# Attention scores from stacked high and low keys over 128 rows, in a decay-attention and two-layer expert kernel

## The chip, the cores and the metric

The kernel runs on one core of one Trainium2 chip. The metric is the device time of one execution in microseconds (us), as the median of several runs. A core has TensorE (PE in the profile, with PEld for its weight loads), VectorE (DVE), ScalarE (ACT), GpSimd (POOL) and SyncE (SP, which issues the DMAs here). All times below come from the runs and from one profiled execution of the kernel before.

## The reference

Decay attention over 4 batches, 8 heads, 576 positions and head size 64; then two expert layers over 2304 tokens (4 x 576), width 512, inner width 2048. Cut to what matters:

```python
def _attn_ref(q, k, v, f):
    scores = (1 / sqrt(64)) * q @ k.T
    cum = np.cumsum(np.log(np.clip(f, 1e-4, 1.0)), axis=-1)
    decay = cum[:, :, :, None] - cum[:, :, None, :]
    scores = np.where(causal, -1e9, scores + decay)
    attn = exp(scores - max(scores)); attn /= sum(attn) + 1e-9
    return attn @ v

def _moe_ref(x, w_in, w_out, alpha):
    h = x @ w_in
    return (np.maximum(h, 0) + alpha * np.minimum(h, 0)) @ w_out

def _moe2_ref(x, w_in, w_out):          # beta = 1
    h = x @ w_in
    return np.where(h >= 1, h, np.where(h <= -1, 0, (h + 1) ** 2 / 4)) @ w_out
```

The expert weights arrive as 64-bit floats and are turned into 32-bit values on the chip.

## The kernel before

**Precision.** PE takes two kinds of 32-bit operands here. Plain F32 products appear in the trace as two products and loads per call; F32R ("fp32r") appear as one. Where F32R is used, each operand is split into a high part (a cast on ACT) and a low part (the difference, on DVE), and three products are summed: high x high, high x low, low x high.

**Attention.** Scores are computed transposed: keys on the 128 output partitions, queries along the columns. Each batch has two units of queries: 0 to 255 ("even") and 256 to 575 ("odd", 320 queries); there are 8 units and each runs over 4 pairs of heads. A pair loads K, Q and V of two heads side by side (2 x 64 = 128 columns), transposes K and Q on PE (L469), copies them out of PSUM on ACT (L476) and, from batch 1 on, makes low parts on DVE (L479). So the two heads of a pair lie on partitions 0 to 63 and 64 to 127, and a score product of one head uses 64 rows only. An even unit has key blocks of 256 and 128 query columns per head, an odd one of 320, 320, 320, 192 and 64. Batch 0 ("plain") uses F32 for everything; in later batches the last block of a head is F32 (L616) and the others are three F32R products (L619). The last key block of an odd unit has 64 keys only.

Per block: score products into one of 2 PSUM buffers, eviction to S on ACT (L633), causal mask on POOL (L420) if it touches the diagonal. Per head: the first block plus its decay bias gives Mx on ACT (L653); each further block is added its bias and maximised into Mx on DVE (L662); POOL reduces Mx over partitions (L669); DVE subtracts bias and maximum from each block (L685); ACT takes the exponential (L690). From batch 1 on, P is split (PH on ACT L700, PL on DVE L704, one buffer each) and multiplied with V (L730 to L732); small blocks and batch 0 use F32 (L724). A column of ones in V gives the sums. Per pair: the results leave PSUM (L766, L767), the sums go through two DMA trips for the reciprocals, DVE multiplies (L795), and ACT and DVE write the high and low parts of the expert input x (L804, L807).

**Expert layers.** Tokens go in 9 chunks of 256, each in 16 slices of the inner width: ps_h (L930, 12 products), the activation on DVE and ACT, ps_y (L988, 12 products); layer 2 is L1077 and L1120. x has a ring of three chunks: x of chunk c can be written only after the ps_h of chunk c-3. Weights are loaded as 64-bit words and converted by ACT and DVE (L849 to L886), 32 pieces a layer; the last 8 pieces of layer 1 go through a ring of 2 staging buffers, and layer 2 opens its buffers when attention has ended. A second memory pool ("phase 2", with split P and V and the split K and Q) opens when layer 1 is converted and batch 0's PV is done.

**Order.** Nothing is ordered by hand. A planner (Order.emit) takes tasks with an engine, an estimated duration, a position, dependencies and buffer rings, and emits each engine's instructions in the order of its own model of time: among the tasks that are ready on an engine, the one with the lowest position. Attention lies ahead of the expert slices by position, so PE takes expert slices when no attention task is ready. Engines then run their queues in that order.

## Time and profile before

| | us |
|---|---|
| median of 3 runs | 1183.98 |
| lowest, highest | 1183.69, 1185.22 |
| the profiled execution | 1185.71 |
| its span, first to last instruction | 1183.9 |

The profile comes from one execution. Busy shares say how long an engine had an instruction in work; the chain of waits follows what ended last back in time; the timeline shows single instructions; a table by stage gives busy times for chosen stretches. Matmul ends are modelled in the profile, so differences between starts, as the chain shows them, are a better measure of a product than its own duration. In the shape of a product, 64\*128 means 64 rows of the array.

### The profile page before, as it was taken

The numbers are of one execution on the slowest core, as the hardware profiler recorded it, in microseconds if no ns is written. First come the engines' busy times: TensorE is split into PE (matmuls) and PEld (weight loads), VectorE is DVE, ScalarE is ACT, GpSimd is POOL, SyncE is SP. The second block draws the span as 40 slices with busy tenths as digits, with TensorE's granted clock in tenths as the row PEclk, the third lists the DMA queues.
The fourth block names the chain that finished last, engine by engine and source line by source line (L and its number), as shares of the span: only waits on it lengthen the run. The fifth ranks groups of instructions, "written<-read, shape, count | busy, mean of one in ns | idle before, by whom it ended". The sixth has DMA issues, their size and how long they took to land.

```text
span 1183.9 us, 20711 instructions
## 1 busy us (share of the span) xinstructions
PE 1126.8 (95%) x7357; PEld 984.6 (83%) x7357; DVE 792.6 (67%) x1892; ACT 615.3 (52%) x1622; POOL 216.9 (18%) x328
## 2 busy tenths in 40 slices
PE   4869988999999999999999998889999999999998
PEld 2436788888888888988889998778999999999997
DVE  4887877677776777657765869997544544444443
ACT  5766754666666657656554435554333333333332
POOL 2512301322332232312210006331000000000000
PEclk9999998999999999999999999999999999999999
DMA  7661122222112122121100623351000010000000
GB/s 198 183 218 36 36 78 78 51 52 55 37 43 74 36 46 49 39 64 42 36 25 8 199 90 120 120 156 38 28 27 19 18 37 19 19 19 1 19 19 18
DMA packets 125656, 72.37 MB, mean 61 GB/s; under 512 B 89424, under 2 KB 119120, under 8 KB 125552
## 3 DMA queue, kind: packets, MB, share of 16 engines
q1 hardware_dynamic: 125552, 71.04, 21.8%
q8 instruction: 58, 0.95, 0.3%
q14 instruction: 46, 0.38, 0.1%
HBM read 61.42 MB, written 9.51 MB: 60 GB/s over the span
## 4 chain that ended last, share of the span: by engine, by line
PE 84%; DVE 8%; DMA 3%; issue 2%; ACT 2%; SPq 1%; POOL 1%; DVEq 0%; ACTq 0%; POOLq 0%
PE ps_h L930 17%; PE ps_y L988 16%; PE ps_z L1120 16%; PE ps_h L1077 15%; PE ps_s L619 6%; PE ps_o L724 5%; PE ps_s L616 4%; PE pst L469 2%; DVE val L867 2%; PE ps_o L730 1%; DVE val L872 1%; DMA raw<-in_moe_w_in_dram 1%; PE ps_o L732 1%; PE ps_o L731 1%; DVE val L852 1%
## 5 line engine op out<-in xcount | busy, mean ns | idle before, releaser
L930 PE MATMUL ps_h<-x,w 128*128 128x256 f32 x1728 | 241.6, 290 | 6.8 <-ACT w L880 4.2
L988 PE MATMUL ps_y<-gH,w 128*128 128x256 f32 x1152 | 240.6, 292 | 3.1 <-ACT gH L948 3.1
L1077 PEld LDWEIGHTS ps_h<-x,w 128*128 128x128 f32 x1728 | 225.5, 191 | 19.2 <-DVE g L1088 8.2
L1077 PE MATMUL ps_h<-x,w 128*128 128x256 f32 x1728 | 230.6, 283 | 4.5 <-DVE g L1088 4.4
L930 PEld LDWEIGHTS ps_h<-x,w 128*128 128x128 f32 x1728 | 219.3, 193 | 16.9 <-ACT w L880 4.4
L988 PEld LDWEIGHTS ps_y<-gH,w 128*128 128x128 f32 x1152 | 189.3, 191 | 12.9 <-issue 4.4
L1120 PE MATMUL ps_z<-w,gH 128*128 128x512 f32 x576 | 180.8, 395 | 0.8 <-ACT gH L1093 0.8
L988 PE MATMUL ps_y<-gL,w 128*128 128x256 f32 x576 | 164.2, 285 | 4.4 <-DVE gL L951 4.3
L1085 ACT ACTIVATE g<-g,half 128x256 f32<-128x256 f32 x144 | 73.3, 509 | 130.7 <-DVE g L1082 130.3
L1096 DVE TENSOR_TENSOR gL<-g,gH 128x256 fp32r<-128x256 f32 x144 | 61.8, 429 | 94.7 <-ACT gH L1093 94.7
L633 ACT COPY S<-ps_s 128x320 f32<-128x320 f32 (+3 forms) x224 | 77.3, 348 | 83.0 <-PE ps_s L619 47.6
L1093 ACT CAST gH<-g 128x256 fp32r<-128x256 f32 x144 | 58.3, 405 | 112.8 <-PE ps_z L1120 104.5
L420 POOL TENSOR_SCALAR_AFFINE_SELECT S<-S 128x128 f32<-128x128 f32 (+1 forms) x160 | 59.1, 375 | 309.9 <-ACT S L633 306.0
L988 PEld LDWEIGHTS ps_y<-gL,w 128*128 128x128 f32 x576 | 110.4, 192 | 6.3 <-DVE gL L951 5.8
L1088 DVE TENSOR_TENSOR g<-ps_h,g 128x256 f32<-128x256 f32 x144 | 61.0, 423 | 81.0 <-ACT g L1085 81.0
L1120 PE MATMUL ps_z<-w,gL 128*128 128x512 f32 x288 | 112.1, 389 | 0.8 <-DVE gL L1096 0.8
L1120 PEld LDWEIGHTS ps_z<-w,gH 128*128 128x128 f32 x576 | 99.0, 190 | 13.6 <-ACT gH L1093 1.0
L669 POOL PARTITION_ALL_REDUCE Mb<-Mx x64 | 85.6, 1338 | 65.5 <-DVE Mx L662 54.7
L685 DVE SCALAR_TENSOR_TENSOR S<-Mb,nb,S 128x320 f32<-128x320 f32 (+3 forms) x224 | 91.5, 457 | 6.0 <-POOL Mb L669 6.0
L724 PE MATMUL ps_o<-S,vF 64*128 64x64 f32 (+4 forms) x256 | 79.1, 401 | 16.9 <-issue 11.4
L948 ACT CAST gH<-g 128x256 fp32r<-128x256 f32 x144 | 58.5, 407 | 68.9 <-DVE g L943 58.7
L662 DVE SCALAR_TENSOR_TENSOR Mx<-S,nb,Mx 128x320 f32<-128x320 f32 (+3 forms) x160 | 69.6, 435 | 33.8 <-POOL S L420 15.2
(96 smaller groups left out, 1679.7 us busy)
## 6 DMA issues: line engine op xcount, KB each, us to landing
raw<-in_moe_w_in_dram SPq DMA_DIRECT2D x32, 512.0 KB
raw<-in_moe_w_out_dram SPq DMA_DIRECT2D x32, 512.0 KB
x<-ysb SPq DMA_DIRECT2D x36, 128.0 KB
x<-x SPq DMA_DIRECT2D x9, 512.0 KB
out_dram<-osb SPq DMA_DIRECT2D x18, 256.0 KB
qr<-in_q_dram SPq DMA_DIRECT2D x64, 64.0 KB
kr<-in_k_dram SPq DMA_DIRECT2D x32, 128.0 KB
vr<-in_v_dram SPq DMA_DIRECT2D x24, 128.0 KB
```

The lines of the kernel that those rows point to most:

```text
L619: nc.tensor.matmul(out=o, lhsT=aa[rows, ks], rhs=qs_.t[cc][rows, qo:qo + m], start=(t == 0), stop=(t == 2))
L633: nc.scalar.copy(out=Sb.t[:, so:so + m], in_=sb.t[:, :m])
L662: nc.vector.scalar_tensor_tensor(out=mo, in0=Sb.t[:, so:so + m], scalar=bias, in1=mo, op0=ALU.add, op1=ALU.max)
L669: nc.gpsimd.partition_all_reduce(Mb.t[:, :n], Mx.t[:, :n], P, ReduceOp.max)
L685: nc.vector.scalar_tensor_tensor(out=sl, in0=Mb.t[:, qo:qo + m], scalar=nb[:, kb, hd:hd + 1], in1=sl, op0=ALU.subtract, op1=ALU.subtract)
L724: nc.tensor.matmul(out=o, lhsT=vf, rhs=Sb.t[:ks, off - g0:off - g0 + m], start=(kb == 0), stop=last)
L930: nc.tensor.matmul(out=hb.t, lhsT=a[:, sl], rhs=b, start=(cc == 0 and t == 0), stop=(cc == NCC - 1 and t == 2))
L988: nc.tensor.matmul(out=Y[c][e // 2][:, e % 2, :], lhsT=a[:, sl], rhs=b, start=(s == 0 and t == 0 and e % 2 == 0), stop=(s == NF - 1 and t ...
L1077: nc.tensor.matmul(out=hb.t, lhsT=a[:, sl], rhs=b, start=(cc == 0 and t == 0), stop=(cc == NCC - 1 and t == 2))
L1085: nc.scalar.activation(out=gb.t, in_=gb.t, func=AF.Square, scale=0.5, bias=half)
L1096: nc.vector.tensor_tensor(out=gg.t[1], in0=gb.t, in1=gg.t[0].bitcast(F32), op=ALU.subtract)
L1120: nc.tensor.matmul(out=zb[tg].t, lhsT=a[:, sl], rhs=b, start=(s == 0 and t == 0), stop=(s == NF - 1 and t == 2))
```

## The change

- K of one head is stacked over 128 partitions: its high part on the head's own 64, its low part on the other 64 (khi, klo). Q is loaded twice per head and transposed once per head, so that each head has the same Q on both halves, split in high and low (qhi, qlo). A score block is then two F32R products of 128 rows, (high and low K) x high Q and (high and low K) x low Q, for every block and every batch; the two F32 forms and the three-product form are gone.
- K buffers: a ring of two, one per head, in the first attention pool. Q: a ring of two there and a third in phase 2. S: six buffers there and a seventh in phase 2, instead of eight.
- The decay bias is added in the eviction (ACT, Identity with a bias per partition). Mx starts as the maximum of the first two blocks on DVE (and, in even units, a copy on ACT of the columns that only the first block has); the later maxima and the subtraction take two tensors and no bias.
- The last key block is padded with zeros to 128 keys, in K, Q, and V, so its transposes and its PV product have 128 rows.
- In the conversion of layer 1, the intermediate values lie in the piece's own weight buffer.
- The planner's estimates for products and for the reduction on POOL are changed.

The diff, cut:

```diff
     def pe(n, cnt=1):
-        return cnt * (max(n, 256) / 2.4 + 3)
+        return cnt * (max(n, 240) / 2.4 + 13)
...
-        raw=2, qr=1, qp=1, q=2, k0=1, k3=1, kF=1, kE=1, S=8, M=3, r=1, PH=1, PL=1, s=2, o=2, h=2, g=4, gg=LH + 1,
-        stage=2, sums=1, rec=1, val=2, raw2=NRAW, val2=NVAL, x2r=1, z0=1, z1=1, osb=3).items()}
+        raw=2, qr=1, q=2, k=2, S=6, M=3, r=1, PH=1, PL=1, s=2, o=2, h=2, g=4, gg=LH + 1,
+        stage=2, sums=1, rec=1, raw2=NRAW, val2=NVAL, x2r=1, z0=1, z1=1, osb=3).items()}
...
+            R["q"].slots.append(None)
+            R["S"].slots.append(None)
...
         def load_q(qb_=qb_, b=b, pr=pr, q0=q0, q1=q1):
-            qb_.t = ap1.tile([P, 3, 2, D], F32, tag="qr", name="qr")
-            load_tok(qb_.t, q, b, pr, q0, q1)
+            qb_.t = QR
+            for x in range(2):
+                load_tok(qb_.t[:, :, :, x, :], q, b, pr, q0, q1)
...
+        kx = [Buf(R["k"]) for _ in range(2)]
...
+            a = last["ktr"] = add("PE", 112 * (t1 - t0) // P, ktr, p0 - 1, [T["lk"], last.get("ktr")],
+                                  new=[pb] + (kx if t0 == 0 else []), use=[kb_] + ([] if t0 == 0 else kx))
+            for j in range(2):
+                hr = slice(j * D, (j + 1) * D)
+                lr = slice(D - j * D, 2 * D - j * D)
+
+                def khi(j=j, hr=hr, pb=pb, t0=t0, t1=t1, k_of=k_of):
+                    nc.scalar.copy(out=k_of(j)[hr, t0:t1], in_=pb.t[hr, :t1 - t0])
+
+                def klo(j=j, hr=hr, lr=lr, pb=pb, t0=t0, t1=t1, k_of=k_of):
+                    nc.vector.tensor_tensor(out=k_of(j)[lr, t0:t1], in0=pb.t[hr, :t1 - t0],
+                                            in1=k_of(j)[hr, t0:t1].bitcast(F32), op=ALU.subtract)
...
-                    for t, (aa, cc) in enumerate(((kx.t[0], 0), (kx.t[0], 1), (kx.t[1], 0))):
-                        nc.tensor.matmul(out=o, lhsT=aa[rows, ks], rhs=qs_.t[cc][rows, qo:qo + m],
-                                         start=(t == 0), stop=(t == 2))
...
+                    for t in range(2):
+                        nc.tensor.matmul(out=sb.t[:, :m], lhsT=kt.t[:, kb * P:(kb + 1) * P],
+                                         rhs=qt.t[t][:, qo:qo + m], start=(t == 0), stop=(t == 1))
...
-                    nc.scalar.copy(out=Sb.t[:, so:so + m], in_=sb.t[:, :m])
+                    nc.scalar.activation(out=Sb.t[:, so:so + m], in_=sb.t[:, :m], func=AF.Identity, bias=bias)
...
+                nc.vector.tensor_tensor(out=Mx.t[:, f0:f0 + fm], in0=S0[0].t[:, S0[1] + f0:S0[1] + f0 + fm],
+                                        in1=S1[0].t[:, S1[1]:S1[1] + fm], op=ALU.max)
...
-                        nc.vector.scalar_tensor_tensor(
-                            out=sl, in0=Mb.t[:, qo:qo + m], scalar=nb[:, kb, hd:hd + 1], in1=sl,
-                            op0=ALU.subtract, op1=ALU.subtract)
+                        nc.vector.tensor_tensor(out=sl, in0=Mb.t[:, qo:qo + m], in1=sl, op=ALU.subtract)
...
-            pool = ph["stage"] if layer == 1 else P2["p"]
-            vb.t = pool.tile([P, DM], F32, tag=f"val{vb.slot}", name="val")
+            pool, tag = (wpool, f"w{i}") if layer == 1 else (P2["p"], f"val{vb.slot}")
+            vb.t = pool.tile([P, DM], F32, tag=tag, name="val")
```

## Rows read from the trace of the kernel before

**Rows 1.** The page, part 1: busy us, share of the span, instructions of each engine.
```profile
PE 1126.8 (95%) x7357; PEld 984.6 (83%) x7357; DVE 792.6 (67%) x1892; ACT 615.3 (52%) x1622; POOL 216.9 (18%) x328
```

**Rows 2.** Busy us by stage: length, engines, granted PE clock, DMA share, GB/s.
```profile
100.00:193.00 93.00, 85.97 (x521) 70.64 (x521) 73.68 (x166) 59.90 (x157) 14.17 (x24) 0.93 0.21 56
193.00:630.00 437.00, 436.36 (x3055) 382.36 (x3054) 311.31 (x823) 280.00 (x835) 121.13 (x228) 1.00 0.20 47
...
705.00:830.00 125.00, 111.64 (x795) 101.73 (x794) 116.03 (x221) 65.05 (x141) 47.74 (x32) 1.00 0.35 106
```

**Rows 3.** Chain of waits, 384 to 399 us: start us, us, engine and line.
```profile
386.82 0.63 PE ps_s L619 x3
387.45 1.62 PE ps_h L930 x12
...
390.47 0.51 PE ps_s L619 x3
...
392.61 0.36 PE ps_s L616 x2
392.97 0.48 PE pst L469 x3
393.45 1.44 PE ps_h L930 x12
...
398.28 0.15 PE ps_o L731
```

**Rows 4.** Timeline: x written (L807, L804), chunks 1 and 6 leaving PSUM (L1005).
```profile
269.11 0.49 DVE L807 TENSOR_TENSOR x<-r,x 128x192 fp32r<-128x192 f32 x2
...
279.28 0.38 ACT L1005 COPY ysb<-ps_y 128x256 f32<-128x256 f32 x1 [0.53 <-PE ps_y L988]
...
353.59 0.55 DVE L807 TENSOR_TENSOR x<-r,x 128x192 fp32r<-128x192 f32 x2
...
600.55 0.41 ACT L804 CAST x<-r 128x256 fp32r<-128x256 f32 x1 [1.24 <-PE ps_h L930]
...
657.17 0.73 DVE L807 TENSOR_TENSOR x<-r,x 128x64 fp32r<-128x64 f32 x2
...
665.33 0.37 ACT L1005 COPY ysb<-ps_y 128x256 f32<-128x256 f32 x1 [0.74 <-PE ps_y L988]
```

**Rows 5.** Chain of waits, 193 to 630 us: shares by line.
```profile
by line: PE ps_y L988 30.4%; PE ps_h L930 30.2%; PE ps_s L619 15.6%; PE ps_o L724 5.4%; PE pst L469 4.5%; PE ps_s L616 4.0%; PE ps_o L730 3.9%; PE ps_o L732 2.9%; PE ps_o L731 2.9%; issue 0.1%; ACT r L767 0.1%; ACT sums L766 0.1%; ACT S L63
```

**Rows 6.** Groups by line, whole span: busy us, mean ns | idle before, releaser.
```profile
L930 PEld LDWEIGHTS ps_h<-x,w 128*128 128x128 f32 x1728 | 219.3, 193 | 16.9 <-ACT w L880 4.4
```

**Rows 7.** Groups by line and form, DVE, 193 to 630 us.
```profile
L685 DVE SCALAR_TENSOR_TENSOR S<-Mb,nb,S 128x320 f32<-128x320 f32 x72 | 36.3, 547 | 0.0
...
L479 DVE TENSOR_TENSOR qL<-pst,qH 128x320 fp32r<-128x320 f32 x12 | 5.8, 484 | 0.3 <-ACT qF L476 0.3
...
L795 DVE TENSOR_TENSOR r<-r,sums 128x320 f32<-128x320 f32 x10 | 4.9, 490 | 6.0 <-DMA sums<-spread 5.9
```

**Rows 8.** Groups by line and form, ACT, 193 to 630 us.
```profile
L633 ACT COPY S<-ps_s 128x320 f32<-128x320 f32 x72 | 30.4, 424 | 32.3 <-PE ps_s L619 30.3 <-DVE PL L704 1.4 <-PE ps_o L724 0.3
...
L653 ACT ACTIVATE Mx<-S,nb 128x320 f32<-128x320 f32 x24 | 13.5, 561 | 0.8
...
L476 ACT CAST qH<-pst 128x320 fp32r<-128x320 f32 x12 | 5.1, 427 | 0.4
```

**Rows 9.** Chain of waits, 91 to 103 us.
```profile
96.48 1.36 PE ps_s L616 x2
...
99.71 2.86 PE ps_h L930 x12
```

**Rows 10.** The end of layer-1 conversion and batch 1's first transposes and x.
```profile
191.45 0.68 DVE L886 TENSOR_TENSOR w<-raw,w 128x512 fp32r<-128x512 f32 x1
...
192.46 0.44 PE pst L469 x4
...
224.94 0.49 DVE L807 TENSOR_TENSOR x<-r,x 128x192 fp32r<-128x192 f32 x2
```

More of the change, by code (lines that the diff above doesn't have):

```diff
@@ L328, in xt @@
         return X[c]
-    assert all(blocks_of(q0, q1)[0][-1][2] <= P for _, q0, q1 in units)
-    KC = 3 * P
+    KC = 4 * P
     V = {}
@@ L356, in open_phase @@
             nc.gpsimd.memset(tf[:, :, 1, :], 0.0 if nm == "vL" else 1.0)
+            if nm == "vF" and S % P:
+                for x in (0, 2):
+                    nc.gpsimd.memset(t[S % P:, cnt - 1, x, :], 0.0)
     open_phase(1)
+    RAW = [ap2.tile([P, NKB, 2, D], F32, name=f"raw{i}") for i in range(2)]
+    QR = ap1.tile([P, 3, 2, 2, D], F32, name="qr")
+    for t in RAW:
+        nc.gpsimd.memset(t[S % P:, NKB - 1], 0.0)
+    nc.gpsimd.memset(QR[S % P:, 2], 0.0)
     def load_tok(dst, src, b, pr, t0, t1):
@@ L454 @@
         T["lk"] = add("SP", 2.85 * nk, load_k, p0 - 3, [last.get("lv"), last.get("lk")], new=[kb_])
         last["lk"] = T["lk"]
-        T["lq"] = last["lq"] = add("SP", 2.85 * n, load_q, p0 - 3, [last.get("lq")], new=[qb_])
-        qs_ = Buf(R["qp" if plain else "q"])
-        def transposes(src, t0, t1, parts, deps, uses, new, pos):
-            m_ = t1 - t0
+        T["lq"] = last["lq"] = add("SP", 5.7 * n, load_q, p0 - 3, [last.get("lq")], new=[qb_])
+        nsplit = sum(y[2] > PVF for y in blocks)
@@ L469, in tr @@
                     nc.tensor.transpose(
-                        pb.t[:, c * P:c * P + m],
-                        src.t[:m, t0 // P + c, :, :].rearrange("p j d -> p (j d)"), ident[:m, :m])
-            a = add("PE", 112 * -(-m_ // P), tr, pos, deps + uses, new=[pb] + new, use=[src])
-            for a0, a1, dstH, dstL, to in parts:
-                def hi(a0=a0, a1=a1, dstH=dstH):
-                    nc.scalar.copy(out=dstH(), in_=pb.t[:, a0:a1])
-                def lo(a0=a0, a1=a1, dstH=dstH, dstL=dstL):
-                    nc.vector.tensor_tensor(
-                        out=dstL(), in0=pb.t[:, a0:a1], in1=dstH().bitcast(F32), op=ALU.subtract)
-                h = add("ACT", act(a1 - a0), hi, pos, [a], use=[pb] + new)
-                to.append(h)
-                if dstL is not None:
-                    to.append(add("DVE", dve(a1 - a0), lo, pos, [h], use=[pb] + new))
@@ new lines, with qtr, qhi, qlo @@
+        qx, qready = [], [[], []]
+        for j in range(2):
+            pb, qb = Buf(R["s"]), Buf(R["q"])
+            qx.append(qb)
+            np_ = -(-n // P)
+            def qtr(pb=pb, qb_=qb_, j=j, np_=np_):
+                pb.t = ps_a.tile([P, 512], F32, tag=f"s{pb.slot}", name="pst")
+                for c in range(np_):
+                    nc.tensor.transpose(
+                        pb.t[:, c * P:(c + 1) * P], qb_.t[:, c, j].rearrange("p x d -> p (x d)"), ident)
+            def qhi(pb=pb, qb=qb, n=n):
+                pool = ap1 if qb.slot < 2 else ph["p"]
+                qb.t = [pool.tile([P, NMAX], F32R, tag=f"q{x}{qb.slot}", name=f"q{x}") for x in "HL"]
+                nc.scalar.copy(out=qb.t[0][:, :n], in_=pb.t[:, :n])
+            def qlo(pb=pb, qb=qb, n=n):
+                nc.vector.tensor_tensor(out=qb.t[1][:, :n], in0=pb.t[:, :n], in1=qb.t[0][:, :n].bitcast(F32),
+                                        op=ALU.subtract)
+            a = add("PE", 112 * np_, qtr, pos_of(2 * pr + j) - 1, [T["lq"], last.get("qtr")], new=[pb], use=[qb_])
+            last["qtr"] = a
+            h = add("ACT", act(n), qhi, pos_of(2 * pr + j) - 1, [a], new=[qb], use=[pb])
+            qready[j] = [h, add("DVE", dve(n), qlo, pos_of(2 * pr + j) - 1, [h], use=[pb, qb])]
@@ L671 @@
             last["par2"] = last.get("par")
-            pa = last["par"] = add("POOL", 400 + 6.3 * n, par, pb_, [mt, last["par2"]], new=[Mb], use=[Mx])
+            pa = last["par"] = add("POOL", 1150, par, pb_, [mt, last["par2"]], new=[Mb], use=[Mx])
             ob = Buf(R["o"])
@@ L722, in pv @@
                         if plain or small:
-                            vf = V["vF"][:ks, kb - v0].rearrange("p a d -> p (a d)")[:, cs]
-                            nc.tensor.matmul(out=o, lhsT=vf, rhs=Sb.t[:ks, off - g0:off - g0 + m], start=(kb == 0), stop=last)
+                            vf = V["vF"][:, kb - v0].rearrange("p a d -> p (a d)")[:, cs]
+                            nc.tensor.matmul(out=o, lhsT=vf, rhs=Sb.t[:, off - g0:off - g0 + m], start=(kb == 0), stop=last)
                             return
@@ L890, in convert @@
         if wide:
-            a = add("ACT", act(DM), mag, pos, [a], new=[vb], use=[rb])
+            a = add("ACT", act(DM), mag, pos, [a] + (wdeps if layer == 1 else []), new=[vb], use=[rb])
             a = add("DVE", dve2(DM), clamp, pos, [a], use=[vb])
```

139 lines of the change are left out of this document (43 added, 96 removed).

## The prediction

> **What bounds the kernel now.** I read the page's busy shares first: PE 95% of the span, DVE 67%, ACT 52% [rows 1]. One mean over stages says little, so the table by stage comes next [rows 2]. From 193 to 630 us, while the attention of batches 1 to 3 is mixed with the first expert layer, PE is busy 436.4 of 437 us, DVE 311 (71%), ACT 280 (64%). From 705 to 830 it is the other way round: DVE 116 of 125 us, PE 112; there the layer-2 weights are converted. Before 193 it is mixed (100 to 193: PE 92%, DVE 79%). So an edit to scores is worth what it takes from PE between 193 and 630, if attention and DVE let the PE have it.
>
> Second, the chain of waits at one place [rows 3]. A 64-row score block (three products, 320 columns) takes 0.63 us, one of 192 columns 0.51, the two-pass-pair small block (L616) 0.36. The third product of a full-row PV triple takes 0.15. Of 0.63 only about 3 x 0.15 = 0.45 is streaming: some 0.18 is paid on entering 64-row mode. The group of 12 expert products behind a score block takes 1.62, but 1.44 behind full-row transposes: 0.18 again on leaving. Neither is a wait on another engine.
>
> Third, who is late at the chunk borders [rows 4]. The last x of unit 2, which chunk 2 needs, is written at 269.1, and chunk 1 leaves PSUM at 279.3; unit 3's last x comes at 353.6. In unit 7, x for chunk 8 is written at 600.6 only after ps_h of chunk 5 frees the ring of three (the row names PE ps_h as releaser), so there the attention waited for PE. The last x comes at 657.2, and chunk 6 leaves its PSUM at 665.3, the 2 to 3 slices by which y trails h: about as at 269. At both places the expert layer had no further chunk to go to: attention is late. PE is thus the limit in the middle, and the attention's own chain at both ends.
>
> **Scores.** Batches 1 to 3 hold 24 heads with 7 blocks each, 168 blocks: 24 of 256 columns, 72 of 320, and 24 each of 192, 128 and 64. The chain gives L619 15.6% and L616 4.0% of 437 us [rows 5], 85.7 us with the entering cost. Leaving adds at most 168 x 0.18 = 30 us, charged to expert and PV groups; I take 27, since few score blocks stand next to another 64-row piece. After the change a block is two full-row products. 320 columns: 2 x 0.146 = 0.29 us [rows 3], 72 x 0.29 = 21 us. For 256 columns and fewer I take 1.44/12 = 0.12 us a product, 96 x 0.24 = 23 us. No row shows an fp32r product of 64 or 128 columns: below, 192 columns are no dearer than that; above, four passes as in L616 would add about 0.1 us to each 128-column product, 5 us in all. I take the former, nearest in form. Sum 44 us.
>
> **Transposes.** K stays at 5 or 2 a pair (the tail padded to 128); Q is transposed per head, from two copies, 6 instead of 3 for an odd unit (320 queries) and 4 instead of 2 for an even one. That is 12 x 3 + 12 x 2 = 60 more, at 0.48/3 = 0.16 us [rows 3]: 9.5 us. So PE loses 85.7 + 27 - 44 - 9.5 = 59 us of work. Per odd pair: 6 x 0.34 + 2 x 0.27 + 2 x 0.12 + 10 x 0.18 - 0.5 = 4.1 us; an even pair keeps the rest, (59 - 49)/12 = 0.8, say 1 us.
>
> The trace puts 12 full-row products, each with its own weights, into 1.44 us, so the loads are hidden [rows 3]. The Trainium skill, "TensorE: Matmul & The Clock Gate", Part 3, What overlaps and what doesn't, says that a weight load overlaps a running product only if the row groups differ, which two full-row products never do. By that rule each of 336 products would show a load, which would eat the gain; here the trace disagrees with it, and the fourth rival prices it.
>
> **DVE.** L479 now makes the low part of K and Q once per head. At 484 ns for 320 columns, 1.5 ns a column [rows 7], an odd pair goes from 832 to 1920 columns (+1.6 us), an even one from 384 to 1024 (+1.0): 31 us in batches 1 to 3. The decay bias leaves L662 and L685, which become two-tensor operations: 547 to about 489 ns at 320 columns [rows 7], 0.058 x 288 = 17 us back. Net +14: 325 of some 390 us, 83%. In batch 0, which had no low parts, it is +18 - 6 = +12 us.
>
> **ACT.** Eviction with bias: 561 instead of 424 ns [rows 8], 168 x 0.137 = +23 us. The first maximum (L653) goes: 48 x some 0.53 = -26 (561 ns at 320 columns, less at 256); even units copy 128 columns instead, 24 x an estimated 0.25 = +6. High parts at 427/320 = 1.33 ns a column: odd 960 to 1920 columns, even 640 to 1024, 21 us. Net +24: 304 of 390 us, 78%.
>
> **SP and buffers.** Q is loaded twice, 80 issues more. From 193 to 630 the DMA share is 0.20 [rows 2], which covers them, and I cost them at nothing (without that cover a pair would wait for its Q); in the first 60 us they stand in SP's order before the v loads that PV waits for, so there they belong to the bound of the start below. S falls from 8 buffers to 6, then 7; two K buffers must both be free before the next pair's transposes, so the longer preparation (ACT +1.3, DVE +1.6 us odd; +0.5, +1.0 even) may stand between the scores of one pair and the next. Queued behind it on ACT are evictions and exponentials, on DVE the low parts of P, and PV waits for those.
>
> **Start, 0 to 193.** Scores of 320 columns take 1.36 us there and 12 expert products 2.86 [rows 9], half pace. PE saves over 20 us, but the stretch ends with the layer-1 conversion: DVE writes the last low part at 191.5, and the PE runs batch 1's transposes at 192.5, behind it [rows 10]. Conversion fills the DVE's gaps, and DVE gets 12 us more. I take 0, between 12 lost (all on the path) and 10 won (attention ends earlier and leaves DVE to conversion).
>
> **193 to 355.** Attention is late here. PE per pair: 4 x 4.1 + 4 x 1 = 20 us; all preparation in series would take back 4 x 2.9 + 4 x 1.5 = 18. So 2 to 20 us; I take 12. Also, K, Q and six S buffers no longer lie in the second pool, so batch 1's first scores need not wait for the conversion, and the 33 us from there to its first x at 224.9 [rows 10] shrink: 0 to 10, I take 6.
>
> **355 to 601.** PE is late. 6 odd and 8 even pairs: 33 us; 28 after some loss to fuller DVE and ACT queues (20 to 33).
>
> **601 to 658.** Chain-bound: 4 us (0 to 8). Afterwards, 2 chunks x 16 slices x 2 x 1.44 = 92 us of expert work and the DVE-bound conversion only shift.
>
> Sum: 0 + 18 + 28 + 4 = 50 us. The profiled execution took 1185.7 (span 1183.9 and 1.8 around it); 1135.7 against it, and as the median of the runs is 1.7 lower, **1134.0 us**.
>
> **The rivals.** (1) PE gets all of it: 59 us, with up to 10 of the start and some of the waiting in 705 to 830 hidden: about 1118. For it: PE idle is nil in 193 to 630, and the 100-to-193 stage keeps PE at 92% with DVE at 79%. Against: the late x at 269 and 657.
>
> (2) Attention's chain or DVE paces everything: only half comes, 1160. For it: DVE at 83% in the mean, and no slack at 269 and 657.
>
> (3) Slower: the longer preparation of K and Q stands in series between pairs and x comes later. Price 18 us before 355 and 3 x 2.9 = 9 us after 601, the middle's gain idle because the next chunk's x is missing: about 1210. It decides when less than 2.9 of the 4.6 us of scores saved per odd pair lies on the attention's chain. Against: score blocks stand in one queue with everything, and the next pair's transposes begin while PV still runs. S at 7 for 8 belongs here: evictions of 320 columns waited only 1.4 us in all for a freed S (releaser DVE PL) [rows 8].
>
> (4) The change doesn't do what it says: loads in the open. A load is 0.193 us long [rows 6], and 336 x 0.193 = 65 us would cancel the 59: 1185 to 1190. The 1.44 us groups speak against it.
>
> **How the numbers follow.** Forecast (1122 to 1148) 0.44, rival 1 0.22, rival 2 0.19, rival 3 0.09, rival 4 0.06. The bounds of all terms give gains of 10 to 81 us; leaving out rivals 3 and 4 and the outer ends, the range is 1106 to 1170. A change of 0.2% (2.4 us) is about what a measurement can tell from none. Faster 0.86, same 0.05, slower 0.09.
>
> **What would show it.** In the chain after: score blocks of 0.29 and 0.24 us, no 64-row form among the products, every group of 12 at 1.44 us, and PE below full in places between 193 and 355. L633 near 560 ns, L685 near 490. Attention's last x near 605 to 610 instead of 657; the end of layer-1 conversion within 12 us of 191. I am wrong if the last x moves by less than 20 us while PE shows gaps (chain-bound), if conversion ends later than 205, or if two full-row products take over 0.4 us.

## The result: slightly slower, 1192.6 us

| | before | after |
|---|---|---|
| median of the runs on the same chip, us | 1184.07 | 1192.56 |
| lowest, highest | 1183.69, 1185.22 | 1192.32, 1194.44 |
| span of the profiled execution | 1183.9 | 1190.9 |

The ratio after to before is 1.0073, 95% interval 1.0056 to 1.0091. The forecast was 1134.0, the range 1106 to 1170. Neither held it; to "slower" the text gave 0.09.

The page of the kernel after, part 1, which answers [rows 1]:

```profile
PE 1063.2 (89%) x7317; PEld 982.2 (82%) x7317; DVE 827.6 (69%) x1992; ACT 635.2 (53%) x1614; POOL 208.8 (18%) x334
```

PE lost 63.6 us of work over the whole run. The forecast had 59 for batches 1 to 3 and "over 20" for batch 0, some 80 together, so the size was too large by some 16 us. Yet the span grew by 7.0, so PE now stands idle for some 71 us more. The table by stage, after, says where (the second, third and fifth line answer [rows 2]; columns as there):

```profile
0.00:100.00 100.00, 47.74 (x161) 33.91 (x162) 75.92 (x174) 63.80 (x149) 24.01 (x45) 0.78 0.68 186
100.00:193.00 93.00, 78.57 (x533) 68.76 (x533) 85.80 (x205) 68.97 (x180) 21.92 (x30) 0.96 0.28 71
193.00:630.00 437.00, 408.15 (x3123) 394.45 (x3123) 327.38 (x882) 289.45 (x809) 113.28 (x223) 0.96 0.23 53
...
600.00:660.00 60.00, 52.02 (x408) 51.30 (x407) 40.19 (x105) 32.04 (x87) 9.97 (x17) 0.93 0.17 46
...
705.00:830.00 125.00, 104.46 (x714) 94.98 (x713) 115.99 (x206) 59.34 (x126) 46.09 (x32) 0.96 0.34 104
830.00:1191.00 361.00, 357.21 (x2261) 323.55 (x2259) 171.99 (x406) 125.24 (x281) 0.00 (x0) 1.00 0.06 20
```

From 193 to 630 PE was busy without a gap before; now it has 29 us of gaps, and in 705 to 830 it works 104.5 us instead of 111.6 while DVE is as full as it was (116.0 in both). The timeline of DVE, after, for the answer to [rows 4] and [rows 10]: the last low part of layer 1's weights (L863), and the last x of units 1, 2 (first pair), 3 and 7 (L784):

```profile
192.73 0.69 DVE L863 TENSOR_TENSOR w<-raw,w 128x512 fp32r<-128x512 f32 x1
...
196.08 0.55 DVE L784 TENSOR_TENSOR x<-r,x 128x256 fp32r<-128x256 f32 x2
...
212.48 0.49 DVE L784 TENSOR_TENSOR x<-r,x 128x192 fp32r<-128x192 f32 x2
...
354.73 0.64 DVE L784 TENSOR_TENSOR x<-r,x 128x192 fp32r<-128x192 f32 x2
...
657.20 0.73 DVE L784 TENSOR_TENSOR x<-r,x 128x64 fp32r<-128x64 f32 x2 [0.36 <-ACT x L781]
```

The last x comes at 657.20; before it came at 657.17 [rows 4]. The attention, with some 60 us less of PE work beside and in it, did not finish earlier at all, and the stretch from the last x to the end grew by 7 us, from 526.7 to 533.7 (span less the start of the last x). The chain of waits after, in one odd pair (batch 1), shows both what worked and what didn't:

```profile
305.38 0.14 PE ps_s L591 x2
305.52 1.51 PE ps_y L965 x12
...
307.47 0.44 PE pst L487 x4
...
308.51 1.49 PE ps_y L965 x12
310.00 1.44 PE ps_h L907 x12
311.44 1.44 PE ps_y L965 x12
...
313.32 0.31 PE ps_s L591 x2
...
315.90 0.29 PE ps_s L591 x2
316.19 1.44 PE ps_y L965 x12
...
318.07 0.29 PE ps_s L591 x2
```

A block of 320 columns takes 0.29 to 0.31 us, as forecast, for 0.63 [rows 3], and the group of 12 behind it 1.44 instead of 1.62. But blocks come 1.7 to 2.6 us apart, since expert groups stand between them, and from the last block of one pair (305.4) over the transposes of the next pair's K (307.5) to its first block (313.3) it is 8 us. An odd pair took 21 to 28 us here (x at 276.8, 302.3, 330.0 and 354.7 in unit 3), where the kernel before needed 19 to 23 (x at 288.4, 307.5, 330.8, 353.6). One pair is not much to go by, so take the nine borders from one odd pair of batches 1 to 3 to the next odd pair. From the start of a pair's last score product to the start of the next pair's first one, the mean is 4.3 us in the kernel before and 9.2 us in the kernel after (from the starts of PE's products in the two traces).

### The profile page after: what moved, and what is told of

The parts are those of the page before. It is cut to its first block, busy times and chain, and to the rows that moved or that the text cites. A ratio compares the mean times of both kernels' runs of the same rounds, so it can differ in the third digit from the quotient of the medians.

```text
span 1190.9 us, 20943 instructions
## 1 busy us (share of the span) xinstructions
PE 1063.2 (89%) x7317; PEld 982.2 (82%) x7317; DVE 827.6 (69%) x1992; ACT 635.2 (53%) x1614; POOL 208.8 (18%) x334
## 4 chain that ended last, share of the span: by engine, by line
PE 59%; DVE 12%; issue 11%; DMA 9%; ACT 4%; SPq 3%; POOL 2%; POOLq 0%; DVEq 0%; ACTq 0%
PE ps_z L1097 16%; PE ps_h L1054 16%; PE ps_h L907 10%; PE ps_y L965 9%; DMA sums<-spread 4%; PE ps_s L591 3%; DVE val L844 2%; DMA spread<-rec 2%; PE ps_o L701 2%; DVE val L829 1%; DMA raw<-in_moe_w_in_dram 1%; SPq L377 1%; DVE val L849 1%; POOL Mb L648 1%; PE ps_o L709 1%
## 5 line engine op out<-in xcount | busy, mean ns | idle before, releaser
L1054 PEld LDWEIGHTS ps_h<-x,w 128*128 128x128 f32 x1728 | 226.6, 192 | 20.7 <-DVE g L1065 9.6
L907 PEld LDWEIGHTS ps_h<-x,w 128*128 128x128 f32 x1728 | 226.9, 198 | 16.2 <-ACT x L781 8.1
L605 ACT ACTIVATE S<-ps_s,nb 128x320 f32<-128x320 f32 (+3 forms) x224 | 99.6, 448 | 46.5 <-PE ps_s L591 44.2
L1065 DVE TENSOR_TENSOR g<-ps_h,g 128x256 f32<-128x256 f32 x144 | 61.1, 424 | 82.5 <-ACT g L1062 82.5
L701 PE MATMUL ps_o<-S,vF 128*128 128x64 f32 (+4 forms) x256 | 72.8, 381 | 26.8 <-ACT r L744 8.2
L591 PE MATMUL ps_s<-qH,kT 128*128 128x320 f32 (+3 forms) x224 | 75.1, 335 | 22.4 <-ACT S L605 8.3
L667 ACT ACTIVATE S<-S 128x320 f32<-128x320 f32 (+1 forms) x192 | 78.1, 423 | 27.6 <-DVE S L664 25.5
L648 POOL PARTITION_ALL_REDUCE Mb<-Mx x64 | 78.2, 1222 | 76.8 <-ACT Mx L632 29.6
```

The lines of the kernel that those rows point to most:

```text
L591: nc.tensor.matmul(out=sb.t[:, :m], lhsT=kt.t[:, kb * P:(kb + 1) * P], rhs=qt.t[t][:, qo:qo + m], start=(t == 0), stop=(t == 1))
L605: nc.scalar.activation(out=Sb.t[:, so:so + m], in_=sb.t[:, :m], func=AF.Identity, bias=bias)
L648: nc.gpsimd.partition_all_reduce(Mb.t[:, :n], Mx.t[:, :n], P, ReduceOp.max)
L667: ex = add("ACT", act(gn), lambda Sb=Sb, gn=gn: nc.scalar.activation(out=Sb.t[:, :gn], in_=Sb.t[:, :gn], func=AF.Exp, scale=-SCALE), pb_, ...
L701: nc.tensor.matmul(out=o, lhsT=vf, rhs=Sb.t[:, off - g0:off - g0 + m], start=(kb == 0), stop=last)
L907: nc.tensor.matmul(out=hb.t, lhsT=a[:, sl], rhs=b, start=(cc == 0 and t == 0), stop=(cc == NCC - 1 and t == 2))
```

## The experiments

Every run of an experiment was compared with the kernel before on the same chip; times are medians, ratios are to the kernel before. The kernel after is at 1.0073. Beside the experiments the kernel before took 1185.8 to 1187.2 us, beside the kernel after 1184.1, so times from different comparisons agree to about 3 us. "The gap" below is the mean over the nine borders just described; "the rest" is the time from the last x to the end of the profiled execution.

**First theory: K's preparation stands in series.** Both K buffers come free only after a pair's last score block. Its rivals, numbered as the expectations of the runs name them and not as in the prediction: (1) seven S buffers for eight; (2) the longer eviction; (3) the second Q load; (4) the planner's estimates; (5) batch 0's preparation on DVE. Four runs.

*K transposed once for each head* (the loop over heads goes outside):

```diff
-        for t0 in range(0, nkp, KC):
+        for j in range(2):
+            for t0 in range(0, nkp, KC):
...
-            a = last["ktr"] = add("PE", 112 * (t1 - t0) // P, ktr, p0 - 1, [T["lk"], last.get("ktr")],
-                                  new=[pb] + (kx if t0 == 0 else []), use=[kb_] + ([] if t0 == 0 else kx))
+                a = last["ktr"] = add("PE", 112 * (t1 - t0) // P, ktr, kpos, [T["lk"], last.get("ktr")],
+                                      new=[pb] + ([kx[j]] if t0 == 0 else []), use=[kb_] + ([] if t0 == 0 else [kx[j]]))
```

> The changed kernel, but K is transposed once for each head, each head's K buffer being freed and refilled by itself. Theory 1 (the preparation of K stands in series between pairs, because both K buffers come free only after the pair's last score block): the next pair's first K is made while the second head's scores run, the gap of some 6.5 us between the score phases of odd pairs (323.5-331.5 scores, next K transposes at 333.5, next scores some 6 us later) shrinks to about 2; 12 odd pairs in batches 1 to 3 would give 12 x 4 = 48 us, of which the expert layer can take no more than PE's idle time from 193 to 630 (437 - 408 = 29 us) less the added transposes (12 x 5 + 12 x 2 = 84 at 0.16 us, 13 us): 1165 to 1180. Rival 1 (seven S buffers for eight) and rival 2 (bias in the eviction lengthens the score ring): the gap is not what paces, 1190 to 1200.

Measured: 1185.94, ratio 0.9991 (0.9972 to 1.001), between the bands of the two theories: some 7 us better than the kernel after, 6 short of what theory 1 wanted. The trace says more than the time. The gap is 5.0 us instead of 9.2 and the last x comes at 638.00, 19 us earlier, as theory 1 has it; but the rest takes 548 us instead of 534, so most of that gain is lost again behind the last x (the edit adds 13 us of transposes to PE).

*Three K buffers, two Q buffers from batch 1 on:*

```diff
-            R["q"].slots.append(None)
+            R["k"].slots.append(None)
```

> The changed kernel with three K buffers from batch 1 on and two Q buffers instead of three (the space allows no more). Both K buffers of a pair are then free as soon as the previous pair's first head has its scores. Theory 1: as K made by head, without its extra transposes: 1160 to 1178. Rival 1 and rival 2: no gain, 1190 to 1200, as K's buffers are not what a pair waits for.

Measured: 1172.16, ratio 0.9881 (0.9844 to 0.9918). The chain of this kernel at the same place:

```profile
306.61 0.29 PE ps_s L591 x2
...
307.23 0.29 PE ps_s L591 x2
...
309.17 0.29 PE ps_s L591 x2
309.46 0.22 PE pst L487 x2
309.68 1.42 PE ps_h L907 x12
...
314.04 0.14 PE ps_s L591 x2
...
316.41 0.24 PE ps_s L591 x2
```

The next pair's K is transposed (L487 at 309.5) while this pair's blocks still run; its first block (0.24 us, so 256 columns: the next unit's) is at 316.4, 2.4 us after the last one. Unit 3's pairs end at 275.2, 301.4, 318.8 and 338.5, so two of them take 17 to 20 us, and the last x comes at 625.55, 32 us earlier. The gap is 4.9 us.

This holds in every kernel of the study, whatever its order. The gap is 3.8 to 4.3 us in the four with the old form of K, 8.5 to 10.8 in the eleven with two buffers that come free together, and 3.6 to 5.8 in the five with a third buffer or K made by head. So two buffers make the gap, and it costs the attention time. What that is worth at the end is another matter: here 32 us at the last x became 20 us in all, since the rest grew from 534 to 545 us.

*Eight S buffers instead of seven, two Q buffers; and the kernel before with six and seven:*

```diff
-            R["q"].slots.append(None)
-            R["S"].slots.append(None)
+            R["S"].slots.append(None)
+            R["S"].slots.append(None)
```

> The changed kernel with eight S buffers from batch 1 on, as before the change, and two Q buffers instead of three. Rival 1 (a head's four S groups, with seven slots, wait for the head before; the kernel before had room for two whole heads): 1165 to 1180, last x before 640. Theory 1: 1189 to 1196, odd pairs stay at 25 us.

Measured: 1193.63, ratio 1.005 (1.003 to 1.0069), last x at 658.9.

> The kernel before with six S buffers, seven from batch 1 on, as in the changed kernel; nothing else. Rival 1: slower by 5 us or more, 1189 to 1205, odd pairs longer than the 20 to 21 us they take before. Theory 1: within 2 us of 1184.

Measured: 1179.56, ratio 0.9935 (0.9912 to 0.9959). In neither kernel did the number of S buffers cost time that could be seen; the first of the two edits also takes one Q buffer away, so only the second tests S alone. The rival has nothing that speaks for it. That the kernel before got faster by 0.65% with less space was expected by no theory, and was the first sign that another order by itself moves the time.

**The parts by themselves.** *The bias part alone, in the kernel before; and the kernel after without it:*

```diff
-                    nc.scalar.copy(out=Sb.t[:, so:so + m], in_=sb.t[:, :m])
+                    nc.scalar.activation(out=Sb.t[:, so:so + m], in_=sb.t[:, :m], func=AF.Identity, bias=bias)
...
-                        nc.vector.scalar_tensor_tensor(
-                            out=sl, in0=Mb.t[:, qo:qo + m], scalar=nb[:, kb, hd:hd + 1], in1=sl,
-                            op0=ALU.subtract, op1=ALU.subtract)
+                        nc.vector.tensor_tensor(out=sl, in0=Mb.t[:, qo:qo + m], in1=sl, op=ALU.subtract)
```

> The kernel before with one part of the change: the decay bias is added in the scores' eviction, the first maximum joins two blocks on DVE, the later maxima and the subtraction become two-tensor operations. S stays at eight, the scores stay 64-row products. If the bias part is harmless (theory 1 puts the loss on K's preparation): 1178 to 1187, L685 near 490 ns, the eviction near 560 ns. Rival 2 (the longer eviction sits in the ring of two score tiles, so every block comes later): 1189 or more, and x of units 3 and 7 later than 353.6 and 657.

Measured: 1176.93, ratio 0.9914 (0.989 to 0.9938). The subtraction at 320 columns, by line and form from 193 to 630 us, takes 494 ns instead of 547 [rows 7]:

```profile
L692 DVE TENSOR_TENSOR S<-Mb,S 128x320 f32<-128x320 f32 x72 | 32.5, 494 | 0.7 <-POOL Mb L676 0.7
```

and the table by stage of the same kernel shows the work taken off: DVE 295.8 us instead of 311.3 [rows 2], ACT 277.8 instead of 280.0.

```profile
193.00:630.00 437.00, 436.62 (x3056) 383.25 (x3056) 295.78 (x817) 277.76 (x807) 118.04 (x222) 1.00 0.19 45
```

> The changed kernel with the bias part taken back: plain eviction, the first maximum on ACT with the bias, the later maxima and the subtraction with the bias as a scalar. Keys stacked, queries held twice, S at six and seven. Theory 1: no faster than the changed kernel, 1189 to 1200 (DVE gets back 17 us of work). Rival 2: 1172 to 1185.

Measured: 1200.38, ratio 1.011 (1.0086 to 1.0134). Both directions go the same way: without the bias part the time is longer. But 8 and 10 us are no more than another order alone can move (below), so that the part helps isn't shown. Nothing shows that the longer eviction costs time, and that rival has nothing that speaks for it.

*K by head with three buffers:* the two edits above together.

> Three K buffers, two Q buffers, and K transposed once for each head, so a head's K can be made one and a half heads ahead. If K's preparation still holds up the attention with three buffers: 1155 to 1168, last x before 615. If DVE and ACT (84 and 76 of 100 us in the stages) pace it by now: 1170 to 1178, as the 84 added transposes of 0.16 us are 13 us more of PE and nothing else moves.

Measured: 1188.6, ratio 1.0016 (0.9999 to 1.0033), last x at 644.8: far from both bands. The finer division with more space is 16 us slower than three buffers alone, although nothing of what theory 1 names is missing: the gap is 5.0 us. Its 84 more transposes are 13 us of PE, and they pass through the two PSUM buffers that the scores use; which of this or the order cost it was not separated.

*Each query loaded once* (scores then hold one half of their terms). The edit also halves the planner's estimate of the load, so the order of the work changes too:

```diff
-            for x in range(2):
-                load_tok(qb_.t[:, :, :, x, :], q, b, pr, q0, q1)
+            load_tok(qb_.t[:, :, :, 0, :], q, b, pr, q0, q1)
...
-        T["lq"] = last["lq"] = add("SP", 5.7 * n, load_q, p0 - 3, [last.get("lq")], new=[qb_])
+        T["lq"] = last["lq"] = add("SP", 2.85 * n, load_q, p0 - 3, [last.get("lq")], new=[qb_])
```

> The changed kernel with each query loaded once: the load of the second copy is left out and its half of the tile stays zero, so a score holds one half of its terms; all instructions on PE, ACT, DVE and POOL stay. Rival 3 (the second Q load and its place in SP's order hold up the next pair's Q, or the r normalisation's transfers behind it): 1170 to 1185. Theory 1: 1188 to 1196, odd pairs stay at 25 us.

Measured: 1173.59, ratio 0.9893 (0.9871 to 0.9916). The odd pairs stay at a mean of 23 to 26 us by unit. The gain comes early: the timeline has the last x of unit 1 at 186.69 instead of 196.08, that of unit 2 at 240.84 instead of 255.65.

```profile
186.69 0.55 DVE L783 TENSOR_TENSOR x<-r,x 128x256 fp32r<-128x256 f32 x2
...
240.84 0.49 DVE L783 TENSOR_TENSOR x<-r,x 128x192 fp32r<-128x192 f32 x2
```

That the load itself costs 19 us isn't shown by this. From 193 to 630 us the kernel after has PE waiting for a query's DMA for 3.2 us in all, this one for 1.0. And a control below, which changes the order and leaves both loads in, brings the last x of unit 1 to the same place:

```profile
186.49 0.56 DVE L784 TENSOR_TENSOR x<-r,x 128x256 fp32r<-128x256 f32 x2
```

*Three K buffers, and the second copy of Q made on GpSimd:*

```diff
-            for x in range(2):
-                load_tok(qb_.t[:, :, :, x, :], q, b, pr, q0, q1)
+            load_tok(qb_.t[:, :, :, 0, :], q, b, pr, q0, q1)
...
+        T["lq"] = add("POOL", pts(-(-n // P) * P), lambda np_=-(-n // P): nc.gpsimd.tensor_copy(
+            out=QR[:, :np_, :, 1, :], in_=QR[:, :np_, :, 0, :]), p0 - 2, [T["lq"]], use=[qb_])
```

> The changed kernel with three K buffers and two Q buffers, and each query loaded once; its second copy is made by GpSimd from the first. If K's buffers and the second Q load are two costs at two places (three buffers shortened the odd pairs from 25 to 18 us, one load brought unit 1's last x from 196 to 187 and unit 2's from 256 to 241): 1155 to 1166. If both only free the same time, because what follows (the layer-2 conversion, or PE) is the limit by then: 1168 to 1176.

Measured: 1149.61, ratio 0.9702 (0.9669 to 0.9735): in this order the two times add up (1192.6 less 20 and 19 would be 1153). The last x comes at 601.47, and the rest takes 546 us.

*Batch 0 with high parts alone:*

```diff
-                    for t in range(2):
+                    if plain:
+                        nc.tensor.matmul(out=sb.t[:, :m], lhsT=kt.t[kr, kb * P:(kb + 1) * P],
+                                         rhs=qt.t[0][kr, qo:qo + m], start=True, stop=True)
+                        return
+                    for t in range(2):
```

> The changed kernel with batch 0's low parts left out: its scores use the high parts alone, one product over 64 rows; batches 1 to 3 are as changed. Takes 12 to 18 us of work from DVE before 193. If batch 0's preparation on DVE delays all that follows (rival 5): unit 1's last x at 176 to 186 instead of 196, the last x earlier by as much, 1178 to 1188. If not: 1189 to 1195.

Measured: 1193.74, ratio 1.0071 (1.0046 to 1.0095), last x at 658.8. DVE's 11 us less between 100 and 193 (74.5 for 85.8) reach nothing.

**The planner's estimates.** The diff's first lines change what the planner believes of a PE product: 240/2.4 + 13 ns instead of 256/2.4 + 3. For a group of 12 expert products that is 1.436 us instead of 1.316; the chain measures 1.44 [rows 3]. So the new value is the nearer one. *All estimates back to the old values, in the kernel after; and the new ones for products and the all-reduce in the kernel before:*

```diff
-        return cnt * (max(n, 240) / 2.4 + 13)
+        return cnt * (max(n, 256) / 2.4 + 3)
...
-                e = last["ev"] = add("ACT", act(m, True) - 50, evac, pb_, [a, nb_ready, last.get("ev")], new=[Sb] if new else [],
+                e = last["ev"] = add("ACT", act(m, True), evac, pb_, [a, nb_ready, last.get("ev")], new=[Sb] if new else [],
...
-            pa = last["par"] = add("POOL", 1150, par, pb_, [mt, last["par2"]], new=[Mb], use=[Mx])
+            pa = last["par"] = add("POOL", 400 + 6.3 * n, par, pb_, [mt, last["par2"]], new=[Mb], use=[Mx])
```

> The changed kernel with the planner's estimates of the kernel before for a PE product, the all-reduce and the biased eviction; the instructions are the same, the order may differ. Rival 4 (the new estimates lay the order badly): 1175 to 1186. Otherwise 1188 to 1197.

Measured: 1178.66, ratio 0.9938 (0.9921 to 0.9956). The last x stays where it was, and the rest falls from 533.7 to 521.6 us:

```profile
659.24 0.73 DVE L784 TENSOR_TENSOR x<-r,x 128x64 fp32r<-128x64 f32 x2 [0.36 <-ACT x L781]
```

> The kernel before with the changed kernel's estimates for a PE product and the all-reduce; instructions the same. It measures how far another order alone moves this kernel. Rival 4: 1189 or more. If the order matters little: 1181 to 1187. A shift of 5 us or more to either side would mean that single differences of that size between these kernels can't be put down to their edit alone.

Measured: 1197.76, ratio 1.0102 (1.0078 to 1.0126). Not one instruction differs from the kernel before, and it is 1% or some 12 us slower; last x at 656.1, but PE works 104.8 us between 705 and 830 instead of 111.6, and the rest takes 540 us instead of 527.

These two runs, with the kernels before and after, are the fair comparison of the change, since each pair has the same estimates. With the old ones the change gains 0.6% (0.9938). With the new ones it gains 0.3 to 0.4% (1192.56 against 1197.76; 1.0073 against 1.0102), which is hardly clear of the noise. The estimates as a whole cost some 12 to 14 us in either kernel, all of it behind the last x.

*The PE estimate alone:* only the first pair of lines of that diff.

> The changed kernel with one old estimate, that of a PE product (256/2.4 + 3 ns instead of 240/2.4 + 13); the all-reduce and the biased eviction stay at the new values. If the PE estimate is what costs some 14 us in both kernels: 1176 to 1183, PE busy in 705 to 830 back at 111 to 113 us. If the all-reduce's or the eviction's estimate does it: 1188 to 1196, 104 to 106 us.

Measured: 1150.43, ratio 0.9697 (0.9669 to 0.9725). The largest single effect of the study, three times what was expected of it, and 28 us below the run with all three estimates old. So the old PE estimate gives its full effect only beside the new ones for the all-reduce and the eviction; whether these two bring the 28 us or another order by itself does was not separated. Its table by stage:

```profile
193.00:630.00 437.00, 412.26 (x3272) 403.27 (x3272) 338.06 (x913) 296.37 (x830) 113.45 (x221) 0.98 0.25 57
...
705.00:830.00 125.00, 115.58 (x772) 103.78 (x772) 100.68 (x207) 57.72 (x127) 29.09 (x21) 1.00 0.27 85
```

In the last line the stretch no longer holds the same work: with x 29 us earlier, the conversion is nearly over at 830, and DVE works 100.7 us of 125. The last x in DVE's timeline, with the idle time ahead of it:

```profile
628.04 0.73 DVE L784 TENSOR_TENSOR x<-r,x 128x64 fp32r<-128x64 f32 x2 [0.36 <-ACT x L781]
```

29 us come before the last x (628.04 for 657.20), 12 behind it. The gap at the pairs' borders is still 8.9 us, so this gain in the attention doesn't come from K's buffers.

*The old PE estimate for chunks 7 and 8 and layer 2 only:*

```diff
+    pe_t = lambda n, cnt=1: cnt * (max(n, 256) / 2.4 + 3)
...
-        th = add("PE", pe(C1, 3 * NCC), h, pos - LH, X_ready[c] + W_ready[1, 2 * s] + [last.get("h")], new=[hb])
+        th = add("PE", (pe_t if c >= 7 else pe)(C1, 3 * NCC), h, pos - LH, X_ready[c] + W_ready[1, 2 * s] + [last.get("h")], new=[hb])
```

> The changed kernel with the old PE estimate for the first layer's chunks 7 and 8 and for layer 2 only; everything up to chunk 7 keeps its order. If the new estimate costs its time in the stretch where the layer-2 weights are converted: last x unchanged near 657, PE busy in 705 to 830 up from 104.5 to 111, 1182 to 1188. If it costs its time in the attention: 1190 to 1195.

Measured: 1176.18, ratio 0.9918 (0.9893 to 0.9944). What PE waited for between 705 and 830, longest first (waited for, us in all, times, longest). First the kernel after:

```profile
PE ps_y L965 <- DVE gL L928: 7.9, 8, 1.8
PE ps_h L1054 <- DVE g L1065: 6.1, 8, 1.4
PE ps_h L907 <- DVE g L920: 4.1, 3, 3.2
```

and the kernel with the old estimate behind chunk 7:

```profile
PE ps_h L1054 <- DVE g L1065: 4.5, 7, 0.9
PE ps_y L965 <- DVE gL L928: 4.1, 4, 1.7
PE ps_h L907 <- DVE g L920: 2.2, 3, 1.2
```

and the latter's stretch in the table by stage:

```profile
705.00:830.00 125.00, 111.85 (x782) 101.18 (x781) 114.28 (x218) 62.55 (x134) 45.65 (x31) 1.00 0.34 106
```

DVE does the same work in both, the conversion of layer 2, and is full. In the one order PE waits 18 us for DVE's activation steps (L928, L920, L1065), in the other 11, and works 7.4 us more: with DVE full in both, those steps come earlier in its queue. The rest takes 522.7 us instead of 533.7. The kernel before shows the same when only its estimates change; what PE waited for between 705 and 830, first with the old estimates, then with the new ones:

```profile
PE ps_h L1077 <- DVE g L1088: 4.4, 7, 0.9
PE ps_y L988 <- DVE gL L951: 4.1, 4, 1.7
PE ps_h L930 <- DVE g L943: 2.5, 4, 1.2
...
PE ps_y L988 <- DVE gL L951: 7.3, 7, 1.8
PE ps_h L1077 <- DVE g L1088: 5.9, 8, 1.4
PE ps_h L930 <- DVE g L943: 4.1, 3, 3.2
```

The last x moved too, from 657.20 to 653.69, though every engine's instructions up to there stand in the same order in both traces: some 3 us is what one execution differs from another.

*Points between:* 12 for 13 ns, 8 for 13 ns, and the old form with 4 for 3 ns.

```diff
-        return cnt * (max(n, 240) / 2.4 + 13)
+        return cnt * (max(n, 240) / 2.4 + 12)
```

> The changed kernel with the PE estimate's constant at 12 ns instead of 13: a control, which changes the order of the work in many places and no instruction. If another order by itself moves the time little: 1189 to 1196. If the time scatters with the order: outside of that, to either side, and single differences of that size are not to be put down to their edit alone.

> The changed kernel with 8 ns instead of 13 in the PE estimate: an expert product is planned at 114.7 ns, between the old estimate's 109.7 (1150 us) and the new one's 119.7 (1192.6; 118.7 gave 1182). If a lower estimate is better as such, because the planner then puts the attention's steps and the layer-2 conversion elsewhere: 1158 to 1176, between the two. If the time only scatters from order to order: it lies outside, or as high as 1185 to 1195.

> The changed kernel with the old form of the PE estimate and 4 ns instead of 3, so an expert product at 110.7. If the low estimate is better as such: 1148 to 1158. If 1150 was one lucky order: 1165 or more.

With the two ends, by what the planner holds of one expert product of 256 columns:

| planned, ns | us | ratio (interval) | last x | the rest |
|---|---|---|---|---|
| 119.7 (after) | 1192.56 | 1.0073 (1.0056 to 1.0091) | 657.2 | 533.7 |
| 118.7 | 1182.35 | 0.9967 (0.995 to 0.9984) | 649.4 | 532.0 |
| 114.7 | 1175.69 | 0.9911 (0.988 to 0.9942) | 645.3 | 527.8 |
| 110.7 | 1165.11 | 0.9829 (0.9811 to 0.9848) | 642.9 | 523.7 |
| 109.7 (as before) | 1150.43 | 0.9697 (0.9669 to 0.9725) | 628.0 | 521.3 |

The time, the last x and the rest all go one way, so with the other two estimates new, the lower PE estimate is better as such in this kernel. But the steps are uneven: one nanosecond is worth 10 us at one end and 15 at the other, and the run with all estimates old, planned at 109.7 as well, has 1178.66 and a last x of 659.2. So the trend behind the last x holds in all of these runs, the one ahead of it only in this row of five. A single difference in the total of some 10 to 15 us can be another order alone, perhaps one of up to 28 us; where a trace shows no more than the total, it can't be put down to its edit.

*Everything together:* three K buffers, the copied Q, and the old PE estimate.

> Three K buffers, two Q buffers, the second copy of a query made by GpSimd, and the old PE estimate. If the three costs (K's two buffers, the second Q load, the order laid by the new estimate) add up: 1149.6 - 14 = 1136, 1131 to 1141. If by now PE's backlog behind the last x is the limit (its 545 us from last x to the end are 12 more than in the changed kernel): 1143 to 1152.

Measured: 1142.86, ratio 0.9632 (0.9603 to 0.9661), last x at 615.75. It is the fastest kernel of the study, 3.7% faster than the kernel before. It isn't the sum: behind the old estimate, K's buffers and the Q load are worth 7.6 us together (1150.43 to 1142.86) and no longer 43, which lies within the scatter. The gap is 5.8 us, the last x 12 us earlier than with the old estimate alone, and the rest takes 526 us instead of 521.

## Why the prediction was wrong, by its steps

**What bounds the kernel** was read rightly for before: PE in the middle, the attention's chain at both ends. What was not drawn from it is that [rows 4] had the last x at 657.2 with the expert layer waiting for it, so a gain on PE is worth nothing until x comes earlier, and that the change lengthened the attention's own chain: the gap between odd pairs went from 4.3 to 9.2 us.

**Scores and transposes.** Block by block the work on PE was sized well: 0.29 to 0.31 us at 320 columns (forecast 0.29), 0.14 at 64 (forecast 0.24, too dear), no 64-row product left. The sum was too large, 63.6 us over the whole run for some 80. One reason shows in the chain: a group of 12 behind a narrow block takes 1.50 or 1.51 us (at 303.4 and 305.5), 0.07 us more than behind a wide one, where the text had 1.44 for every group. The fourth rival, loads in the open, falls at 320 columns. The Trainium skill's rule ("TensorE: Matmul & The Clock Gate", Part 3, What overlaps and what doesn't), by which two full-row products never hide each other's load, isn't what these blocks show: two of them with two loads take 0.29.

**DVE** grew by 16 from 193 to 630 (forecast 14) and 12 between 100 and 193 (forecast 12 for batch 0). The two-tensor subtraction takes 489 ns at 320 columns, as forecast. **ACT** grew by 9 in the middle instead of 24. The eviction with bias took 525 ns, not 561, which is about 6 us of it; the high parts of K and Q grew by some 14 us in batches 1 to 3 instead of 21 (an estimate, three quarters of what their lines take over the whole run). By line and form, after:

```profile
L605 ACT ACTIVATE S<-ps_s,nb 128x320 f32<-128x320 f32 x72 | 37.8, 525 | 19.2 <-PE ps_s L591 18.7
...
L664 DVE TENSOR_TENSOR S<-Mb,S 128x320 f32<-128x320 f32 x69 | 30.0, 489 | 8.9 <-POOL Mb L648 8.8
```

**SP and buffers.** K's two buffers are a step that failed. The text said that the preparation "may stand between the scores of one pair and the next", took 8 us off for it before 355 (of 18, if all of it stood in series at 2.9 us an odd pair) and 5 us for fuller queues from 355 to 601. The gap grew by 4.9 us a border, as a mean over the three odd units, and a third buffer took it back and brought the last x 32 us earlier. The second Q load, of which the text says "I cost them at nothing", stays open: leaving it out gave 19 us in this order, the copy on GpSimd 22.5 on top of three K buffers, but an order with both loads in had unit 1's last x as early. S at seven showed no cost, as forecast.

**Start.** The conversion's end moved from 191.45 to 192.73, the forecast's 0, and batch 1's first x came 12.5 us earlier (212.48 for 224.94 [rows 10]; forecast 6, at most 10). But unit 1's last x came 21 us later (196.1 after), more than the 12 us that the start's bound allowed. In the kernel before:

```profile
175.34 0.56 DVE L807 TENSOR_TENSOR x<-r,x 128x256 fp32r<-128x256 f32 x2
```

**193 to 355, 355 to 601, 601 to 658.** The gains of 18, 28 and 4 us are missing entirely: unit 3's last x 354.73 for 353.59, the last one 657.20 for 657.17. This is the sum's failed step: it took work saved on PE as time, 50 us of it, while the attention's chain, which delivers x, did not get shorter. Two things were found that hold it up, each by taking it away: the gap that K's two buffers make (a third buffer: last x 625.55) and, in one set of estimates, the order of the queues (the old PE estimate: 628.04). Both together give 615.75, so they overlap. The prediction gave its own sign for this ("the last x moves by less than 20 us while PE shows gaps"), and that is what happened.

**The planner's estimates** are in the diff and no step of the prediction speaks of them. This is a second failed step, a term put at nothing without a reason. All estimates taken back give 14 us (1178.66), and in the kernel before the new ones alone cost 1%. These 12 to 14 us lie behind the last x, in the conversion of layer 2, where the order alone was changed and the loss went away; they are more than the 8.5 us by which the kernel after is slower. With only the line of the PE estimate taken back, the changed kernel runs at 1150.4, inside the range that the text gave and 16 us above its forecast. The other 29 us of that gain lie in the attention and come only in this set of estimates, so they are no proof that the forecast's mechanism was right.

**Rival 3** (slower by preparation in series) named a mechanism that the trace shows, the 8 us from a pair's last block to the next pair's first, and its sign came true. Its price of 27 us was about what three buffers gave back (20 us in all, 32 at the last x); its number, 1210, was not reached. With the old PE estimate the two-buffer kernel is fast as well, with the gap still at 8.9 us. So it is a cause, but not the only one. **Rival 2**, half the gain, put the time at 1160 and is closest to what the kernel does with the old PE estimate.

**What stays open.** Why a planner that holds products for 8% shorter than they are lays the better order. In the stretch of the layer-2 conversion the trace shows where the time goes (PE's waits for activation steps on a full DVE); for the attention only the effect is shown, and only with the new estimates for the all-reduce and the eviction beside it. How much of the time K's buffers, the Q load and the order cost each can't be told apart below the scatter. Nor was it tested what the estimates of the all-reduce and the eviction do by themselves.

## What to carry to other kernels

Where a program lays out the queues from estimated durations, an estimate is part of the change: cost the order, not only the instructions, and run the old kernel with the new estimates and the new one with the old before anything is put down to an instruction. Work taken off the busiest engine is worth time only as far as the chain beside it gets shorter too; look at the last arrival of what that chain delivers (here the last x), before and after. Where one nanosecond in an estimate moves the time by 10 us, a trend over several points is evidence and a single difference in the total isn't; a quantity of the mechanism itself, such as the gap between two pairs, can still tell the kernels apart.

## What was not expected of the hardware

A full-row score block of 64 columns, two products with a load each, took 0.14 us in the chain, half of one of 320 columns (0.29), and the group of 12 behind it 1.51 us instead of 1.44. The eviction from PSUM with a bias took 525 ns where the biased pass over SBUF had taken 561 [rows 8] and the plain eviction 424. Low parts of K written across the partition halves, 64 partitions by 512 columns, took 689 ns on DVE; a subtraction over 128 partitions by 512 columns (w, L863) took 0.69 us at 192.7, so half the height brought nothing. From 193 to 630 us, where PE now had gaps, the granted clock was 0.96 instead of 1.00 [rows 2], so part of PE's busy time there is the same work at the lower of its two levels.
